# Four copies per head pair moved from GpSimd to VectorE in a fused attention and MLP-mixer kernel

## The chip, the cores and the metric

The kernel runs on one core of one Trainium2 chip. The metric is the device time of one execution in microseconds (us), smaller is better. The times quoted are medians of several executions; the profiled span is about 2 us shorter than the time of the same execution.

The engines of a core that matter here are TensorE (PE in the profile: matmuls; PEld: its weight loads), VectorE (DVE), ScalarE (ACT), GpSimd (POOL), which in this kernel also issues all input transfers, and the DMA engines that carry them out. Each engine has its own list of instructions, whose order is set when the program is built.

## The reference, cut to what matters

```python
# attention: 4 batches, 8 heads, 768 positions, head size 64; 8 global keys, window of 96
scores = q @ k.transpose(0, 1, 3, 2) / sqrt(D)
keep = is_global | is_local                  # key < 8, or 0 <= query - key < 96
scores = where(keep, scores + bias, -1e9)    # bias: -slope[head] * distance
a = softmax(scores);  x = a @ v              # reshaped to (4, 768, 512)
# mixer
u  = x + (x^T @ U @ V)^T                     # low rank 32 over positions
out = u + relu(u @ w_ch1) @ w_ch2            # 512 -> 2048 -> 512
```

Inputs and output are float32; the kernel computes in float16.

## The kernel before

The kernel takes two heads of one batch together, so there are 16 pairs. Of the 768 x 768 scores it computes only 128 x 128 blocks: six on the diagonal (from `kT`, the transposed keys) and five next to it (from `kP`). `kP` is a copy of `kT` whose first 32 columns of each block are overwritten with the first 32 keys, so that one matmul covers the previous block and the global keys. `vp` is the same for the values. Each is made by two copies, all four on GpSimd:

```python
            kT = qkp.tile([P, NSB, P], FP16, name="kT", tag="kT")
            nc.vector.tensor_copy(kT.rearrange("p n c -> p (n c)"), tp)        # from PSUM
            kP = qkp.tile([P, NPB, P], FP16, name="kP", tag="kP")
            nc.gpsimd.tensor_copy(kP[:, :, G:P], kT[:, 0:NPB, G:P])
            nc.gpsimd.tensor_copy(
                kP[:, :, 0:G], kT[:, 0:1, 0:G].broadcast_to((P, NPB, G))
            )
# ... (in mask(i), after the products with the exponential mask)
        nc.gpsimd.tensor_copy(vp, vh[:, :, 0:NPB])
        nc.gpsimd.tensor_copy(vp[0:G], vh[0:G, :, 0:1].broadcast_to((G, 2, NPB, D1)))
```

All inputs are converted from float32 to float16 by their transfer, which GpSimd issues:

```python
    def load_pair(i):                       # 2 transfers each of q, k, v
        # ...
                nc.gpsimd.dma_start(stg[:, :, hi], src[b, 2 * hp + hi].rearrange(...))
        # ...
    load_pair(0)
    # ... constants; load_pair(1); constants
    load_pair(2)
    load_pair(3)
    # ... u16, v16w (the low-rank weights)
    for c in range(NDC):
        nc.gpsimd.dma_start(w1_16[:, c], w1v[:, c])
    load_pair(4)
    for c in range(0, NJC, 2):
        nc.gpsimd.dma_start(w2_16[:, c:c + 2], w2v[:, c:c + 2])
    load_pair(5)
    # ... then one load_pair(i + 6) per step of the main loop
```

The main loop overlaps, per step, the low-rank mix of one pair, the attention of the next, and the scores of the one after. When all four pairs of a batch are done, that batch's MLP matmuls are queued and fill TensorE's gaps in the later steps. A scheduler sets the final order on every engine. In the names of the profile, `qkst` is a staging tile of q or k, `v_81` the values, `sc` scores, `ob` the attention output, `hps` and `cps` the two MLP products, `w_16_79` and `w_16_80` the MLP's weights.

The softmax here doesn't subtract the row's maximum and nothing guards it: scores larger than these inputs give would overflow.

## Time and profile before

| | before |
|---|---|
| time, median of 2 runs | 336.53 us (336.28 to 336.78) |
| profiled span | 334.3 us |
| TensorE busy | 263.7 us (79%) |
| VectorE / ScalarE / GpSimd busy | 114.4 / 132.1 / 126.5 us |

The first view gives the busy time of each engine in stretches of the span that I chose at events: until the first score matmul, until the scores of pair 2, until the MLP matmuls start in bulk, and the rest. After the length of the stretch come the busy times (with counts) of TensorE, its weight loads, VectorE, ScalarE and GpSimd, the granted TensorE clock (as a share of its full rate), the time that the transfers' packets took as a share of the 16 DMA engines' time (the times of packets are added up, so it can exceed 1), and GB/s. The clock column also says 1.00 where the trace has no record of the clock, which is so for the first three stretches.

```profile
core 0: us, PE busy (x) PEld busy (x) DVE busy (x) ACT busy (x) POOL busy (x), PEclk, DMA share, GB/s
0.00:50.81 50.81, 3.20 (x24) 2.47 (x25) 3.47 (x11) 4.69 (x9) 41.75 (x64) 1.00 1.43 143
50.81:68.76 17.95, 11.00 (x119) 8.39 (x120) 10.67 (x23) 8.28 (x15) 15.71 (x22) 1.00 1.33 85
68.76:108.96 40.20, 31.08 (x270) 20.95 (x271) 19.09 (x47) 18.09 (x32) 23.41 (x33) 1.00 0.79 51
108.96:334.30 225.34, 218.45 (x1668) 117.17 (x1667) 81.12 (x176) 100.98 (x210) 45.60 (x68) 1.00 0.29 42
```

Read the TensorE column against the length. In the first 50.81 us TensorE works 3.2 us. In the last 225.34 us it works 218.45: there TensorE is the bound, and only there.

The timeline shows what the first stretch waits for (start, duration, engine, line and operation; in brackets the idle time of the engine before it and what ended it). These are the first eviction of `kT`, one of the transfers, the first `kP` and the first score matmul.

```profile
9.48 0.56 DVE L182 COPY kT<-tp 128x768 f16<-128x768 f16 x1 [0.89 <-PE tp L170]
...
32.41 0.82 POOL L100 DMA_DIRECT2D v_81<-in_v_dram  x1 [1.59 <-DMA w_16_79<-in_moe_w_ch_dram]
...
49.90 0.60 POOL L184 COPY kP<-kT 128x480 f16<-128x480 f16 x1
...
50.81 0.71 PE L206 MATMUL sc<-qT,kP 64*128 64x128 f16 x9 [36.76 <-POOL kP L185]
```

`kT` of pair 0 is there at 10.04 us, and GpSimd makes `kP` of it at 49.90. Apart from four short mask operations (11.95 to 13.06 us), GpSimd was not computing in the meantime: in its fixed order, the transfers of pairs 0 to 5 and of all weights stand ahead, and some of these wait for earlier transfers to land, as the bracket at 32.41 us says. (By the trace the issues use eight semaphores in turn: those held up from 29.99 us on wait for the transfer eight before them, and at most eight are in flight.) The list of waits gives the total (us, number of waits, longest):

```profile
PE sc L206 <- POOL kP L185: 44.9, 7, 36.8
```

In the third stretch the same thing happens at a smaller scale, once per pair:

```profile
88.92 0.56 DVE L182 COPY kT<-tp 128x768 f16<-128x768 f16 x1 [1.35 <-PE tp L170]
...
89.12 1.66 POOL L94 DMA_DIRECT2D qkst<-in_k_dram  x2
...
90.75 0.62 POOL L184 COPY kP<-kT 128x480 f16<-128x480 f16 x1
91.28 0.35 POOL L185 COPY kP<-kT 128x160 f16<-128x160 f16 x1
...
91.68 0.71 PE L206 MATMUL sc<-qT,kP 64*128 64x128 f16 x9 [1.35 <-POOL kP L185]
```

`kT` is ready at 89.48, but GpSimd is issuing two k transfers until 90.78 and finishes `kP` at 91.63; TensorE was idle 1.35 us. The four groups of copies, with total busy us and mean ns of one:

```profile
L232 POOL COPY vp_82<-v_81 128x650 f16<-128x650 f16 x16 | 12.1, 758 | 1.3 <-PE ob L252 1.3
L233 POOL COPY vp_82<-v_81 32x650 f16<-32x650 f16 x16 | 12.1, 754 | 0.4
L184 POOL COPY kP<-kT 128x480 f16<-128x480 f16 x16 | 9.9, 621 | 49.5 <-DVE kT L182 49.5
...
L185 POOL COPY kP<-kT 128x160 f16<-128x160 f16 x16 | 5.6, 352 | 0.0
```

### The profile page before, as it was taken

Reading aid. Unit: us, or ns where it says so; the run is one execution under the profiler, and the core shown is the slowest. Engines: PE = TensorE matmul, PEld = TensorE weight load, DVE = VectorE, ACT = ScalarE, POOL = GpSimd, SP = SyncE. Lnnn points to the kernel's source line nnn. Section 1 sums busy time; section 2 is a strip of 40 time slices with the busy share of each in tenths; the row PEclk is TensorE's granted clock in tenths of the full one; section 3 lists DMA queues with packets and bytes.
Section 4 is the critical chain, followed back from the end, with each engine's and each line's share of the span. In section 5 each row is a group of like instructions: output and inputs, shape, how many; then the busy total and the mean of one; then the engine's idle time right before and its main releaser. Section 6 shows DMA issues by size and latency. Waiting matters only on the chain.

```text
span 334.3 us, 5123 instructions
## 1 busy us (share of the span) xinstructions
PE 263.7 (79%) x2080; PEld 149.0 (45%) x2080; DVE 114.4 (34%) x255; ACT 132.1 (39%) x265; POOL 126.5 (38%) x185
## 2 busy tenths in 40 slices
PE   0200006667688999999999999999999999999995
PEld 0200004545455556554455654555655554555442
DVE  0300004744544433355452434556342353100111
ACT  0320005353344485714447672415576521377100
POOL 8997579757645527143614140210201000000000
PEclk9999999999999999999999999999999999999999
DMA  9999999889749659258907160011000011100021
GB/s 70 96 120 184 181 205 116 53 55 73 48 33 64 40 32 59 14 65 102 113 32 49 9 42 33 31 65 63 2 0 2 2 63 63 65 0 0 33 92 65
DMA packets 82326, 20.34 MB, mean 61 GB/s; under 512 B 76640, under 2 KB 78720, under 8 KB 82304
## 3 DMA queue, kind: packets, MB, share of 16 engines
q0 software_dynamic: 78848, 13.74, 52.3%
q1 hardware_dynamic: 3456, 6.29, 5.1%
q8 instruction: 16, 0.26, 0.3%
q14 instruction: 6, 0.05, 0.1%
HBM read 27.46 MB, written 6.29 MB: 101 GB/s over the span
## 4 chain that ended last, share of the span: by engine, by line
PE 61%; POOL 16%; ACT 9%; DMA 6%; issue 4%; DVE 3%; POOLq 0%; ACTq 0%
PE cps L348 25%; PE hps L329 22%; POOL qkst L94 7%; PE sc L206 5%; ACT htr L335 4%; POOL v_81 L100 4%; DMA w_16_79<-in_moe_w_ch_dram 3%; PE h_ps L294 3%; ACT ep L212 3%; DMA w_16_80<-in_moe_w_ch_dram 3%; PE tmp_ps L282 2%; PE tp L170 2%; DVE x_sb L299 1%; POOL kP L184 1%; ACT uu L303 1%
## 5 line engine op out<-in xcount | busy, mean ns | idle before, releaser
L329 PE MATMUL hps<-uT,w_16_79 128*128 128x384 f16 x512 | 97.8, 330 | 2.7 <-ACT htr L335 0.7
L348 PE MATMUL cps<-w_16_80,htr 128*128 128x512 f16 x384 | 91.1, 379 | 0.0
L335 ACT ACTIVATE htr<-hps 128x384 f16<-128x384 f32 x128 | 58.0, 497 | 48.2 <-PE hps L329 48.2
L212 ACT ACTIVATE ep<-sc 128x512 f16<-128x512 f32 (+1 forms) x96 | 49.1, 583 | 62.4 <-PE sc L206 62.4
L329 PEld LDWEIGHTS <-w_16_79 128*128 128x128 f16 x512 | 49.2, 97 | 38.8 <-issue 8.7
L224 DVE TENSOR_TENSOR ep<-ep,expb 128x640 f16<-128x640 f16 x64 | 29.7, 498 | 73.7 <-ACT ep L212 73.6
L348 PEld LDWEIGHTS <-htr 128*128 128x128 f16 x384 | 34.5, 98 | 36.7
L94 POOL DMA_DIRECT2D qkst<-in_q_dram x32 | 26.9, 856 | 62.9 <-PE tp L170 61.9
L206 PE MATMUL sc<-qT,kP 64*128 64x128 f16 x160 | 13.2, 251 | 45.5 <-POOL kP L185 44.9
L354 DVE TENSOR_TENSOR osb<-cps,x_sb 128x512 f32<-128x512 f32 x24 | 16.5, 689 | 57.7 <-PE cps L348 57.5
L206 PEld LDWEIGHTS <-kP 64*128 64x128 f16 x160 | 6.6, 106 | 54.8 <-POOL kP L185 47.5
L170 PE MATMUL tp<-ident_91,qkst 128*128 128x128 f16 x192 | 21.1, 256 | 10.9 <-POOL ident_91 L113 7.2
L94 POOL DMA_DIRECT2D qkst<-in_k_dram x32 | 26.8, 860 | 6.5 <-PE ob L252 3.3
L184 POOL COPY kP<-kT 128x480 f16<-128x480 f16 x16 | 9.9, 621 | 49.5 <-DVE kT L182 49.5
L100 POOL DMA_DIRECT2D v_81<-in_v_dram x32 | 26.7, 847 | 3.8 <-DMA w_16_79<-in_moe_w_ch_dram 1.9
L303 ACT ACTIVATE uu<-x_sb 128x768 f16<-128x768 f32 x16 | 13.5, 844 | 37.1 <-DVE x_sb L299 36.7
L170 PEld LDWEIGHTS <-qkst 128*128 128x128 f16 x192 | 15.9, 115 | 16.1 <-issue 11.5
L299 DVE TENSOR_TENSOR x_sb<-x_sb,h_ps 128x768 f32<-128x768 f32 x16 | 15.3, 955 | 19.6 <-PE h_ps L294 19.6
L206 PE MATMUL sc<-qT,kT 64*128 64x128 f16 x192 | 20.7, 251 | 0.1
L252 PE MATMUL ob<-v_81,ep 128*128 128x65 f16 x160 | 17.6, 209 | 0.0
L248 PE MATMUL ob<-vp_82,ep 128*128 128x65 f16 x160 | 16.9, 210 | 0.0
L182 DVE COPY kT<-tp 128x768 f16<-128x768 f16 x16 | 8.9, 558 | 22.1 <-PE tp L170 18.7
(103 smaller groups left out, 210.0 us busy)
## 6 DMA issues: line engine op xcount, KB each, us to landing
out_dram<-osb SPq DMA_DIRECT2D x24, 256.0 KB, 2.0
qkst<-in_q_dram POOLq DMA_DIRECT2D x32, 96.0 KB, 3.7
qkst<-in_k_dram POOLq DMA_DIRECT2D x32, 96.0 KB, 3.6
v_81<-in_v_dram POOLq DMA_DIRECT2D x32, 96.0 KB, 3.6
w_16_79<-in_moe_w_ch_dram POOLq DMA_DIRECT2D x4, 512.0 KB, 8.5
w_16_80<-in_moe_w_ch_dram POOLq DMA_DIRECT2D x8, 256.0 KB, 7.7
u_151<-in_moe_U_dram POOLq DMA_DIRECT2D x1, 48.0 KB, 3.9
v16w<-in_moe_V_dram POOLq DMA_DIRECT2D x1, 48.0 KB, 3.5
```

What stands on the lines that cost most here:

```text
L94: nc.gpsimd.dma_start(stg[:, :, hi], src[b, 2 * hp + hi].rearrange("(n p) d -> p n d", p=P),)
L100: nc.gpsimd.dma_start(v16[:, i % VR, hi, :, 0:D], v[b, 2 * hp + hi].rearrange("(n p) d -> p n d", p=P),)
L170: nc.tensor.matmul(tp[:, sb * P:(sb + 1) * P], stg[:, sb].rearrange("s h d -> s (h d)"), ident16, is_transpose=True, start=(sb == 0), stop ...
L206: nc.tensor.matmul(scs[hi][:, j * P:(j + 1) * P], lhsT, qT[r, t * P:(t + 1) * P], start=(j == 0), stop=(j == len(idx) - 1),)
L212: nc.scalar.activation(ep[:, hi, idx[0]:idx[0] + n].rearrange("p n c -> p (n c)"), scs[hi][:, 0:n * P], AF.Exp, scale=qk_scale,)
L224: nc.vector.tensor_tensor(blk, blk, expb[:, h, m:m + 1].broadcast_to((P, NPB, P)), ALU.mult)
L248: nc.tensor.matmul(ob[:, t], ep[:, hi, t - 1], vp16[:, i % 2, hi, t - 1], start=True, stop=False,)
L252: nc.tensor.matmul(ob[:, t], ep[:, hi, NPB + t - 1], v16[:, i % VR, hi, t], start=False, stop=True,)
L299: nc.vector.tensor_tensor(xp, xp, hps[:, 0:S].rearrange("p (n c) -> p n c", n=NSB), ALU.add)
L329: nc.tensor.matmul(hh[f][:, 0:HT], w1_16[:, dc, jt * P:(jt + 1) * P], uTs[b][:, dc, f * HT:(f + 1) * HT], start=(dc == 0), stop=(dc == NDC ...
L335: nc.scalar.activation(htr[:, jt, f * HT:(f + 1) * HT], hh[f][:, 0:HT], AF.Relu)
L348: nc.tensor.matmul(cps, htr[:, jc, tt * P:(tt + 1) * P], w2_16[:, jc], start=(jc == 0), stop=(jc == NJC - 1),)
```

## The change

The intent is to leave GpSimd nothing but transfers, so that no copy waits behind a transfer.

```diff
-            nc.gpsimd.tensor_copy(kP[:, :, G:P], kT[:, 0:NPB, G:P])
-            nc.gpsimd.tensor_copy(
+            nc.vector.tensor_copy(kP[:, :, G:P], kT[:, 0:NPB, G:P])
+            nc.vector.tensor_copy(
                 kP[:, :, 0:G], kT[:, 0:1, 0:G].broadcast_to((P, NPB, G))
             )
 ...
-        nc.gpsimd.tensor_copy(vp, vh[:, :, 0:NPB])
-        nc.gpsimd.tensor_copy(vp[0:G], vh[0:G, :, 0:1].broadcast_to((G, 2, NPB, D1)))
+        nc.vector.tensor_copy(vp, vh[:, :, 0:NPB])
+        nc.vector.tensor_copy(vp[0:G], vh[0:G, :, 0:1].broadcast_to((G, 2, NPB, D1)))
```

## The prediction

This was written before the changed kernel had run.

> **What bounds the kernel now.** Three stages, by the table of engine time per stretch. (1) 0 to 50.8 us: TensorE is busy 3.2 us. (2) 50.8 to 109: attention pairs 0 to 4, one per 11.46 us, TensorE busy 42.1 of 58.2 us. (3) 109 to 334.3: MLP matmuls fill the gaps, TensorE busy 218.4 of 225.3 us and the bound.
>
> Stage 1 is no lack of data. By the timeline kT of pair 0 is ready at 10.0 us, of pair 1 at 14.7, but kP (GpSimd) starts at 49.9: GpSimd works in order, and ahead of kP stand the transfers of pairs 0 to 5 and all weights, which from about 29 us wait for earlier ones to land. The waits view names it: the score matmul waited 36.8 us for kP. In stage 2 kP stands behind two k transfers (kT ready 89.5, kP 91.6 us).
>
> **What the change does.** It takes 64 copies off GpSimd (per pair 0.62 + 0.35 + 0.76 + 0.75, in all 39.7 us) and adds 64 to VectorE (34% busy). The Trainium skill ("VectorE: DVE Perf Modes", the perf-mode tier table) gives an fp16 SBUF copy 4 elements a cycle. This trace has no such copy; its fp32 one (128x128, 217 ns) fits that page's 2 a cycle plus about 150 cycles. With that fixed part I estimate 0.28 + 0.19 + 0.33 + 0.33 = 1.1 us per pair, 18 in all. The transfers keep their order until 50 us, then have fewer gaps. TensorE's order moves little.
>
> **On the critical path.** Stage 1: kP(0) by 10.6 us, scores at once; the masks' table on ScalarE ends at 17.3 as before, exponentials of pairs 0 and 1 by 23, attention-times-value 23.5, normalisation 25, low-rank mix 27 (its weights issued 22.7, landing about 3.9 later). Scores of pair 2 start at about 32 us, not 68.8. Stage 2: going through one period with measured durations, kP is ready 1.4 us sooner, but the normalisation waits for two copies more and exponentials go ahead of x16: 10.2 us per pair instead of 11.46. Scores of pair 5 at 32 + 3 x 10.2 = 62.7 us (before 103.1), MLP from 68.6 (before 109). Transfers of pairs 4 and 5 should land near 37 and 53 us, in time. Stage 3 stays 225.3, less 1.5 for gaps where kP stood behind transfers (159 to 164 us). Sum: 68.6 + 223.8 + 2.2 (time over span) = 294.6.
>
> **Prediction: 295 us, 8 in 10 between 287 and 307.** Faster by over 2%: 0.96; within 2%: 0.03; slower: 0.01.
>
> **What would show it.** The long wait for kP is gone; scores of pair 0 start near 11 us, of pair 2 near 32; period 10.2 us; MLP from 69 us; TensorE's idle time falls by 41 us, its busy time stays 264; VectorE's busy time rises by 18 us.
>
> **What would make it wrong.** (a) The skill ("SBUF — State Buffer", Who interferes with whom) says a two-port VectorE copy and GpSimd exclude each other, and that issuing transfers suffers. Here the 217 ns copy ran inside a GpSimd issue undelayed, so I expect little; were it total, copies and issues of 0.85 us would stretch and early transfers slip. (b) The copies miss the fast mode (0.65 us for vp): 5 us more. (c) Later transfers land late, and TensorE, in order, stalls ahead of stage 3. (d) VectorE's longer queue delays evictions in stage 3, where each microsecond of TensorE counts. (e) A lower granted clock once TensorE works without pause.

## The result, and the profile after

| | before | after |
|---|---|---|
| time, median of 2 runs | 336.53 us | 295.70 us (295.11 to 296.29) |
| ratio | | 0.8787 (95% interval 0.8706 to 0.8867) |
| TensorE busy / idle in the span | 263.7 / 70.6 us | 262.6 / 31.9 us |
| VectorE busy | 114.4 us | 132.3 us |
| GpSimd busy | 126.5 us | 89.9 us |
| scores of pair 0 / 2 / 5 start | 50.8 / 68.8 / 103.1 us | 12.3 / 32.6 / 64.2 us |
| MLP matmuls start in bulk | 108.96 us | 69.26 us |
| from there to the end of the span | 225.34 us | 225.24 us |

A ratio is the mean time of one kernel's runs over that of the other's of the same rounds, so it is not quite the ratio of the medians. The idle time of TensorE is the span less its busy time.

The stretches between the same events as before:

```profile
core 0: us, PE busy (x) PEld busy (x) DVE busy (x) ACT busy (x) POOL busy (x), PEclk, DMA share, GB/s
0.00:12.27 12.27, 2.32 (x18) 1.83 (x19) 2.09 (x6) 1.28 (x1) 11.22 (x21) 1.00 1.26 80
12.27:32.60 20.33, 12.39 (x125) 9.06 (x125) 13.37 (x38) 10.63 (x22) 18.17 (x27) 1.00 1.50 138
32.60:69.26 36.66, 28.60 (x272) 20.47 (x271) 24.47 (x65) 17.83 (x33) 28.18 (x36) 0.98 1.74 161
69.26:294.50 225.24, 219.33 (x1670) 117.89 (x1668) 92.34 (x212) 100.81 (x209) 32.36 (x40) 0.99 0.37 47
```

The whole gain, 334.3 - 294.5 = 39.8 us of span, lies ahead of the MLP: its start moves by 108.96 - 69.26 = 39.7 us. The last stretch keeps its length to 0.1 us, although VectorE now works 92.34 us in it instead of 81.12. The early timeline (pair 0's `kT`, its first `kP` copy, the q transposes of pair 1, pair 0's scores):

```profile
9.46 0.56 DVE L182 COPY kT<-tp 128x768 f16<-128x768 f16 x1 [0.89 <-PE tp L170]
10.06 0.44 DVE L184 COPY kP<-kT 128x480 f16<-128x480 f16 x1
...
11.54 0.80 PE L170 MATMUL tp<-ident_91,qkst 128*128 128x128 f16 x6 [2.11 <-DMA qkst<-in_q_dram]
...
12.27 0.71 PE L206 MATMUL sc<-qT,kP 64*128 64x128 f16 x9
```

`kP` starts 0.04 us after `kT` is done. The scores then wait for a different thing: TensorE's order has pair 1's q transposes first, and these waited 2.11 us for their transfer. The line that answers to the third stretch of before:

```profile
39.82 2.82 POOL L155 DMA_DIRECT2D w_16_80<-in_moe_w_ch_dram  x4
...
40.67 0.56 DVE L182 COPY kT<-tp 128x768 f16<-128x768 f16 x1 [1.19 <-PE tp L170]
...
41.26 0.31 DVE L184 COPY kP<-kT 128x480 f16<-128x480 f16 x1
...
41.49 0.47 DVE L185 COPY kP<-kT 128x160 f16<-128x160 f16 x1
...
42.01 0.71 PE L206 MATMUL sc<-qT,kP 64*128 64x128 f16 x9
```

While GpSimd issues weight transfers, `kT` ends at 41.23, both copies at 41.96, and the scores start at 42.01, with no idle time of TensorE named. The copies on VectorE:

```profile
L233 DVE COPY vp_82<-v_81 32x650 f16<-32x650 f16 x16 | 6.7, 425 | 0.1
L184 DVE COPY kP<-kT 128x480 f16<-128x480 f16 x16 | 6.7, 419 | 0.4
L232 DVE COPY vp_82<-v_81 128x650 f16<-128x650 f16 x16 | 6.4, 407 | 12.9 <-PE ob L252 8.4 <-DMA v_81<-in_v_dram 4.5
...
L185 DVE COPY kP<-kT 128x160 f16<-128x160 f16 x16 | 4.5, 280 | 0.1
```

Two things in these lines had not been foreseen. The means add to 1.53 us per pair, not 1.1. And `vp` (L232) now has idle time of VectorE ahead of it, 4.5 us of which ended with a transfer of v. That is one single wait:

```profile
52.00 0.55 DVE L317 COPY uT<-tpu 128x768 f16<-128x768 f16 x1
57.03 0.51 DVE L232 COPY vp_82<-v_81 128x650 f16<-128x650 f16 x1 [4.48 <-DMA v_81<-in_v_dram]
...
58.28 0.47 DVE L224 TENSOR_TENSOR ep<-ep,expb 128x640 f16<-128x640 f16 x1
58.67 0.27 DVE L286 CAST tmp_748<-tmp_ps 32x128 f16<-32x128 f32 x1
...
59.00 0.79 PE L294 MATMUL h_ps<-tmp_748,v16w 32*128 32x128 f16 x6 [3.32 <-DVE tmp_748 L286]
```

From 52.5 to 57.0 us VectorE stands still for a `vp` copy. It is the copy of pair 5: its v, the last of the early transfers, was issued at 49.3 and 50.7 us. The scheduler put this copy ahead of the masks (L224) of pair 4 and of the low-rank eviction (L286) of pair 3, whose inputs were there by 54.4 and 55.2 us. So TensorE, too, stood still: 3.32 us for that eviction. The scores follow each other at 32.60, 42.01, 51.42 and 64.23 us: 9.41, 9.41 and then 12.81 us.

### The profile page after: what moved, and what is told of

The parts are those of the page before. It is cut to its first block, busy times and chain, and to the rows that moved or that the text cites. A ratio compares the mean times of both kernels' runs of the same rounds, so it can differ in the third digit from the quotient of the medians.

```text
span 294.5 us, 5117 instructions
## 1 busy us (share of the span) xinstructions
PE 262.6 (89%) x2080; PEld 149.2 (51%) x2080; DVE 132.3 (45%) x319; ACT 130.6 (44%) x265; POOL 89.9 (31%) x121
## 4 chain that ended last, share of the span: by engine, by line
PE 67%; DMA 9%; POOL 9%; ACT 7%; DVE 4%; issue 2%; POOLq 0%; ACTq 0%; DVEq 0%
PE cps L348 28%; PE hps L329 27%; DMA w_16_79<-in_moe_w_ch_dram 4%; POOL qkst L94 4%; PE sc L206 3%; ACT htr L335 3%; DMA w_16_80<-in_moe_w_ch_dram 3%; POOL v_81 L100 2%; DMA v_81<-in_v_dram 2%; PE tpu L311 2%; DVE x_sb L299 2%; PE h_ps L294 2%; PE tmp_ps L282 2%; ACT ep L212 2%; PE tp L170 2%
## 5 line engine op out<-in xcount | busy, mean ns | idle before, releaser
L329 PE MATMUL hps<-uT,w_16_79 128*128 128x384 f16 x512 | 96.5, 330 | 2.0
L212 ACT ACTIVATE ep<-sc 128x512 f16<-128x512 f32 (+1 forms) x96 | 48.5, 582 | 41.1 <-PE sc L206 41.1
L224 DVE TENSOR_TENSOR ep<-ep,expb 128x640 f16<-128x640 f16 x64 | 28.9, 485 | 33.5 <-ACT ep L212 33.1
L206 PE MATMUL sc<-qT,kT 64*128 64x128 f16 x192 | 21.4, 244 | 4.0 <-ACT ep L212 3.9
L206 PEld LDWEIGHTS <-kT 64*128 64x128 f16 x192 | 11.5, 104 | 15.0 <-issue 13.1
L270 DVE TENSOR_TENSOR x_sb<-ob,rcp 128x384 f32<-128x384 f32 x32 | 16.2, 547 | 0.0
L248 PEld LDWEIGHTS <-ep 128*128 128x128 f16 x160 | 13.7, 108 | 4.4 <-issue 2.7
## 6 DMA issues: line engine op xcount, KB each, us to landing
w_16_79<-in_moe_w_ch_dram POOLq DMA_DIRECT2D x4, 512.0 KB, 10.2
```

Of the source, the lines that this page charges most:

```text
L206: nc.tensor.matmul(scs[hi][:, j * P:(j + 1) * P], lhsT, qT[r, t * P:(t + 1) * P], start=(j == 0), stop=(j == len(idx) - 1),)
L212: nc.scalar.activation(ep[:, hi, idx[0]:idx[0] + n].rearrange("p n c -> p (n c)"), scs[hi][:, 0:n * P], AF.Exp, scale=qk_scale,)
L224: nc.vector.tensor_tensor(blk, blk, expb[:, h, m:m + 1].broadcast_to((P, NPB, P)), ALU.mult)
L248: nc.tensor.matmul(ob[:, t], ep[:, hi, t - 1], vp16[:, i % 2, hi, t - 1], start=True, stop=False,)
L329: nc.tensor.matmul(hh[f][:, 0:HT], w1_16[:, dc, jt * P:(jt + 1) * P], uTs[b][:, dc, f * HT:(f + 1) * HT], start=(dc == 0), stop=(dc == NDC ...
```

## The experiments

Theory: the gain comes from leaving GpSimd's in-order queue, in which copies stood behind transfers; the speed of the copies hardly matters, since the MLP stage is bound by TensorE and takes 225 us whatever comes before it. Rival: VectorE's copies are faster (1.5 us per pair instead of 2.5), and the gain goes with the copy time moved. A second question is what the change costs: VectorE's time, the new wait for v, and the stretched copies. The times below are medians of four or five runs; "before" ran beside each at 336.7 to 337.0 us.

### Only kP moves

```diff
-            nc.gpsimd.tensor_copy(kP...   (both)
+            nc.vector.tensor_copy(kP...   (both); vp stays on GpSimd
```

> Only the two kP copies move to VectorE; the two vp copies stay on GpSimd, behind the transfers. Queue theory (the gain comes from leaving GpSimd's in-order queue of transfers): scores of pairs 0 and 1 start near 12 and 18 us as with the whole change, but the first attention-times-value matmul now waits for vp until about 51 to 53 us, so only some 5 us of the early gain and 1 to 2 us per pair later are kept: 323 to 331 us, the gains of the two halves do not add up. Speed rival (VectorE's copies are simply faster, 1.5 against 2.5 us per pair): a gain in proportion to the copy time moved, about 4/10 of 41 us, 318 to 321 us.

Measured 324.75 us, ratio 0.9639 (0.9613 to 0.9666). The scores of pair 0 and 1 started at 12.18 and 18.91 us, as with the whole change, and the first matmul that needs `vp` waited:

```profile
PE ob L248 <- POOL vp L233: 29.9, 1, 29.9
```

So the half that made the scores 38 us early gained 12 us, because the next step then waited in the same queue. The queue theory's range held; the rival's 318 to 321 did not.

### Only vp moves

```diff
-        nc.gpsimd.tensor_copy(vp...   (both)
+        nc.vector.tensor_copy(vp...   (both); kP stays on GpSimd
```

> Only the two vp copies move; kP stays on GpSimd. Queue theory: the score matmul still waits for kP until about 50 us, stage 2 gains at most 1 us per pair: 328 to 336 us. Speed rival: 6/10 of 41 us gained, 310 to 314 us.

Measured 335.85 us, ratio 0.9967 (0.9941 to 0.9993). The scores of pair 0 started at 51.92 us. This half moves 1.5 of the 2.5 us of copies per pair and gains 1 us. The halves gain 12 and 1 us, both together 41: each removes one of two waits that end at nearly the same time (in the kernel before GpSimd starts `kP` at 49.90 us and `vp` at 50.69), and only removing both lets the chain go on. The rival would have had them add up.

### The copies stay on GpSimd, the transfers come later

```diff
-    load_pair(2); load_pair(3); <u16, v16w, w1>; load_pair(4); <w2>; load_pair(5)
 ...  in the loop, after mask(i + 1):
+        if i == -1: load_pair(2); load_pair(3); <u16, v16w>
+        if i == 0: <w1>
+        if i in (2, 3): <half of w2>
+        if 0 <= i < NP - 4: load_pair(i + 4)
```

> All four copies stay on GpSimd, but the program issues the transfers of pair 2 onwards and of the weights inside the loop, after the copies they used to stand before; the same transfers and copies, no copy on VectorE. Queue theory: scores of pair 0 start near 13 us and most of the gain appears without VectorE: 297 to 312 us (some lost since copies still stand behind weight transfers here and there and the pair chain keeps its 11.5 us). Speed rival, or that only VectorE frees GpSimd's 40 us: 325 to 340 us.

Measured 303.65 us, ratio 0.9009 (0.898 to 0.9037): 33 us gained with no copy on VectorE, and the groups of copies unchanged (0.61, 0.35, 0.76 and 0.74 us). The order of the queue is enough for most of the gain. The timeline shows what is still missing (`kT` is L172 here, `kP` L174):

```profile
12.94 0.64 POOL L174 COPY kP<-kT 128x480 f16<-128x480 f16 x1
...
14.24 0.48 DVE L172 COPY kT<-tp 128x768 f16<-128x768 f16 x1
...
26.24 0.67 POOL L174 COPY kP<-kT 128x480 f16<-128x480 f16 x1
...
27.23 0.71 PE L196 MATMUL sc<-qT,kP 64*128 64x128 f16 x9 [3.14 <-POOL kP L175]
```

Pair 0's `kP` is made at 12.94 us, but pair 1's, whose `kT` was ready at 14.72, at 26.24: the transfers of pairs 2 and 3 and the small weights still stood ahead.

### The same program with the copies on VectorE

```diff
 (e3_gp_loads_later)
-            nc.gpsimd.tensor_copy(...   (all four)
+            nc.vector.tensor_copy(...
```

> The program of e3_gp_loads_later (transfers issued inside the loop) with the four copies on VectorE: against e3 only the engine of the copies differs. Queue theory: with the transfers no longer ahead of the copies the engine itself is worth little, what is left being kP behind single transfers and pair 1's scores (27.2 us in e3): 4 to 9 us, 295 to 300 us. Speed rival: the move to VectorE is worth most of its 41 us here too: under 285 us; or nothing at all, 302 to 305 us.

Measured 292.5 us, ratio 0.8692 (0.8671 to 0.8713). That is 11 us less than with GpSimd, more than the 4 to 9 expected, and 2.5 us below the range. The difference is there early: scores of pair 1 at 18.91 instead of 27.23 us, of pair 2 at 32.50 instead of 40.45 (8 us), MLP at 65.35 instead of 75.46. By these times some 8 of the 11 us are again the queue, of which e3 had left more than I counted: in e3 pair 1's `kP` still waited there. Another 2 us come by the start of the MLP, and 1.7 after it (the last stretch takes 225.0 us instead of 226.7). How much of that is the shorter copies is not separated.

### Pair 5's transfers ahead of the second weight matrix

```diff
 (kernel after)
+    load_pair(5)
     for c in range(0, NJC, 2):
         nc.gpsimd.dma_start(w2_16[:, c:c + 2], w2v[:, c:c + 2])
-    load_pair(5)
```

> The kernel after, with pair 5's six transfers issued before those of the second weight matrix. Theory: in the kernel after, VectorE's vp copy of pair 5 stands ahead of pair 4's masks and waits 4.5 us (52.5 to 57.0 us) for v of pair 5, and pair 5's period is 12.8 us instead of 9.4. With v there in time that wait goes, MLP starts near 66 us, and 2.5 to 4 us are gained: 291.5 to 293.5 us. Rival (the longer period comes from elsewhere, or the saved time is lost to TensorE-bound stage 3): within 1 us of the kernel after, 295 to 297 us.

Measured 292.92 us, ratio 0.8692 (0.8669 to 0.8715). The wait is gone:

```profile
52.18 0.55 DVE L317 COPY uT<-tpu 128x768 f16<-128x768 f16 x1
52.64 0.32 DVE L232 COPY vp<-v 128x650 f16<-128x650 f16 x1
...
54.63 0.49 DVE L224 TENSOR_TENSOR ep<-ep,expb 128x640 f16<-128x640 f16 x1 [1.00 <-ACT ep L212]
```

The copy now starts at 52.64, right after the eviction ahead of it, and the masks wait 1.00 us for ScalarE only. Pair 5's scores come 8.99 us after pair 4's instead of 12.81, MLP starts at 66.13 us, and the last stretch takes 291.2 - 66.13 = 225.1 us. The wait for v was worth what it looked to be worth.

### Each copy made twice

```diff
 (kernel after)
             nc.vector.tensor_copy(kP[:, :, G:P], kT[:, 0:NPB, G:P])
+            nc.vector.tensor_copy(kP[:, :, G:P], kT[:, 0:NPB, G:P])
 ...  the same for the other three
```

> The kernel after with each of the four VectorE copies made twice (same result): another 64 copies, about 20 to 25 us of VectorE time. Theory: VectorE's time counts only in the chain of stage 2, where the second kP copy delays the scores by 0.5 us or a little more per pair, and stage 3 stays 225 us: 297.5 to 301 us in all. Rival A (VectorE's time counts in full, so the change paid its 18 us somewhere): 312 us or more. Rival B (VectorE time costs nothing at all): 295 to 296.5 us.

Measured 300.06 us, ratio 0.8903 (0.887 to 0.8936): 4.4 us above the kernel after (4.1 above e9 below, which ran in the same rounds) for another 64 copies, inside the theory's range and far from 312. In the profiled run MLP starts at 70.98 us, 1.7 later than in the kernel after, and the last stretch takes 225.9 us. That run was the fastest of the four (298.66); where the slower ones lose 1 to 2 us more is not known.

### kP copied from PSUM

```diff
 (kernel after)
-            nc.vector.tensor_copy(kP[:, :, G:P], kT[:, 0:NPB, G:P])
+            nc.vector.tensor_copy(kP[:, :, G:P], <tp as (p, n, c)>[:, 0:NPB, G:P])
 ...  the same for kP[:, :, 0:G]
```

> The kernel after, but the two kP copies read the transposed k in PSUM instead of kT in SBUF[...]. Port theory (the stretching of these copies from 0.31 to up to 0.71 us and from 0.19 to up to 0.79 us comes from GpSimd's issues holding the shared port): each copy then has one length, near 0.41 and 0.26 us, also inside GpSimd's issues; the total time stays within 1.5 us of the kernel after, 294.5 to 297 us. Rival (they stretch for another reason, such as waiting for the instruction before): the spread of lengths stays as in the kernel after.

Measured 295.98 us, ratio 0.8787 (0.8764 to 0.8809), the kernel after's. The lengths of one copy (minimum, median, maximum in ns) in the kernel after:

```profile
L184 DVE COPY kP<-kT x16: 307/309/711, 10.1 to 214.3; 128x480 f16<-128x480 f16 x16
L185 DVE COPY kP<-kT x16: 184/193/785, 10.4 to 214.5; 128x160 f16<-128x160 f16 x16
```

and here:

```profile
L184 DVE COPY kP<-tp x16: 386/398/400, 9.9 to 213.6; 128x480 f16<-128x480 f16 x16
L185 DVE COPY kP<-tp x16: 219/231/231, 10.2 to 213.9; 128x160 f16<-128x160 f16 x16
```

With a PSUM source the copies have one length to within 14 ns, as the port theory expected: the Trainium skill ("SBUF — State Buffer", Who interferes with whom) says that VectorE's two-port modes share a port pair with GpSimd, and that a VectorE instruction with one SBUF input at most, outside those modes, does not contend. The trace of the kernel after points the same way for all four groups: 22 of its 64 copies are longer than the others of their group (over 0.34 us, or 0.2 for L185), and each of them overlaps a transfer issue of GpSimd; the 19 that overlap none, `vp` copies among them, all have the short length. (A PSUM source was not tried for `vp`.) It makes no difference in time here: the copies from PSUM vary less, but their median is longer (398 instead of 309 ns, 231 instead of 193).

### The low-rank weights earlier

```diff
 (e4_w2_late)
+    <u16, v16w>
     load_pair(2)
     load_pair(3)
-    <u16, v16w>
```

> e4_w2_late with the two small low-rank weights issued before pair 2 instead of after pair 3. In the kernel after the first low-rank matmul waited 3.3 us for them (to 26.5 us) while its other operand was ready at 24.7. Theory: some 1.8 us earlier from there on, all of it kept as stage 3 stays 225 us: 290 to 291.8 us. Rival (pairs 2 and 3, now 1.5 us later, or something else then ends last): as e4, 292.5 to 293.5 us.

Measured 292.8 us, ratio 0.87 (0.8673 to 0.8727): no gain over e4_w2_late, so the expectation failed. The scores of pair 2 to 5 did come earlier (pair 5: 59.06 instead of 60.59), but then:

```profile
DVE vp L232 <- DMA v<-in_v_dram: 2.3, 1, 2.3
PE h_ps L294 <- DVE tmp L286: 1.8, 1, 1.8
```

The hoisted `vp` copy, now of pair 6, waited 2.3 us for its v, which stood behind the second weight matrix, and TensorE waited 1.8 us for the low-rank eviction behind that copy. The MLP started at 65.48 us, only 0.65 earlier. The same wait had moved to the next pair.

### The constants earlier

```diff
 (e7_uv_early)
+    <identity, distances, ones column of v>; q and k of pair 0; <distance masks>; v of pair 0
-    load_pair(0); <identity, distances>; load_pair(1); <distance masks, ones column of v>
+    load_pair(1)
```

> e7_uv_early with the constants (identity, distance table, ones column of v) built before v of pair 0 instead of around pair 1. In the kernel after ScalarE's table of exponentials ended at 17.4 us and pair 0's exponentials only then went on, to 19.9. Theory: the table ends near 10 to 11 us, pair 0's exponentials near 16, and 2 to 4 us more are gained than by e7: 286.5 to 289.5 us; stage 3 still 225 us. Rival: the early stage is then bound by arriving pairs, and it gains under 1 us over e7.

Measured 293.05 us, ratio 0.8695 (0.8662 to 0.8728). This failed too. VectorE's `vp` copies waited 8.1 us for v in four places before 70 us, and MLP started at 65.87.

### Transfers in the order of their use

```diff
 (e7_uv_early and, for e12, e10_consts_first)
     for c in range(NDC):
         nc.gpsimd.dma_start(w1_16[:, c], w1v[:, c])
+        if c < 2:
+            load_pair(4 + c)
-    load_pair(4); load_pair(5); <w2>
 ...  in the loop, after load_pair(i + 6):
+            if i in (1, 2): <half of w2>
```

> e7_uv_early with the transfers of pairs 4 and 5 set between the chunks of the first weight matrix and the second weight matrix split behind pairs 7 and 8 (that is, as late as possible). In e7 VectorE's vp copy of pair 6 waited 2.3 us for v of pair 6, which came behind the second weight matrix, and the MLP started at 65.5 us though the scores of pair 5 were 1.5 us earlier than in e4. Theory (the same hoisted-copy wait, moved one pair on, ate e7's gain): with v earlier the wait goes, MLP starts near 64 us, stage 3 stays 225 us: 290 to 292 us. Rival (stage 3 grows by as much as the MLP starts earlier): as e7, 292.5 to 293.5 us.

> The same order of transfers with the constants of e10 first. In e10 VectorE's vp copies waited 8.1 us in four places for v behind weights, which ate its earlier start. Theory: without those waits the MLP starts near 61 to 63 us: 287 to 290.5 us. Rival: as e10, 291.5 to 293.5 us.

e11_interleaved: 291.3 us, ratio 0.8657 (0.8639 to 0.8675); MLP from 63.86 us, then 225.24. One wait of `vp` for v, of 2.2 us, was still there before 70 us. e12_interleaved_consts: 290.07 us, ratio 0.8616 (0.8599 to 0.8634); such waits add to 2.0 us there (8.1 in e10), MLP from 63.13 us, then 225.27. Both are in their ranges except that e12's MLP starts 0.1 us later than expected. e12 is the best version found: 5.6 us less than the kernel after. It also shows the limit of this road: in these runs the start of the MLP is nearly all that the transfers' order moved.

Across the profiled runs the start of the MLP explains the span: before 108.96, only kP 96.78, only vp 108.75, after 69.26, e4 66.13, e12 63.13 us, and the rest of the span is 225.1 to 225.7 us in each of them (226.7 with the copies on GpSimd and late transfers, 225.9 with doubled copies, 226.1 in e10).

## Why the prediction was right, point by point

- **Time.** 295 us predicted, 295.7 measured. The mechanism, the queue ahead of `kP`, is shown by e1 to e3: the same copies on GpSimd with the transfers behind them gain 33 of the 41 us. TensorE's idle time fell by 38.7 us, where 41 had been predicted.
- **Stage 1.** Scores of pair 2 at 32 us, measured 32.6. The first scores came at 12.3, not 10.6: I had overlooked that pair 1's q transposes stand ahead on TensorE and wait for their transfer. ScalarE had its table to finish until 17.4 us anyway, so little hung on it: in e9 they start at 10.54 us, those of pair 1 at 18.87 as here, and the time is the same.
- **Stage 2.** 10.2 us per pair predicted. Two pairs took 9.41, the third 12.81, together 31.63 us against 30.6. The number was nearly right by two errors: the undisturbed period was shorter than I worked out, and the named risk (c), late transfers, came true in a form I had not seen: VectorE waited first, for a copy that the change had put into its queue, and TensorE 3.32 us for VectorE. e4 shows its price, 2.8 us (295.7 to 292.9).
- **Stage 3.** I had taken 1.5 us off for gaps where `kP` stood behind transfers. That was wrong: the stretch is 225.24 us against 225.34. Fewer such waits did not shorten it. Which other waits took their place I did not follow up.
- **VectorE.** Busy time rose by 17.9 us, with 18 predicted, but the copies took 1.53 us each pair, not 1.1. Undisturbed ones came close to the estimates (0.31, 0.19, 0.32 and 0.32 us against 0.28, 0.19, 0.33 and 0.33); the rest is copies that stretched during transfer issues, for `kP` by the shared port (e9). Risk (a) was real, and as far as e9 tests it harmless. The agreement on 18 us is partly luck: the sum of the copies' lengths is 24.3 us, the lengths of neighbouring VectorE instructions overlap in the profile, and the masks (L224, L227) are together about 2 us shorter than before. Moving the copies causes this: between e3 and e8, which differ in the copies' engine alone, the masks also go from 35.6 to 33.4 us. How is open: of the six that are clearly lengthened in the kernel before, five overlap a GpSimd copy, but of the five in e3 three overlap only transfer issues.
- **Transfers.** They kept their order, as predicted, but not quite their times: the first v of pair 4 was issued at 31.73 instead of 29.99 us, for the first MLP weights landed later. In e1 it was 30.01, in e2 31.26. Whether the `vp` copies do that is left open; one profile each does not settle it.
- **Clock.** Risk (e) did not come. The profile's mean of 0.91 between 60 and 80 us is one stretch at 0.50, from 68.1 to 71.5 us, the same half rate that TensorE had before its first clock record (last section). Lasting full rate starts 2.2 us after the MLP's start here and 2.6 us after it in the kernel before, so it follows the earlier start and does not explain it.

## What to carry to other kernels

Ask of every small instruction on an engine that also issues transfers what stands ahead of it in that engine's order: here 40 us of a 336 us kernel were small copies, each under 0.8 us, standing behind transfers they did not need. Moving such work to another engine moves its waits there too, so look afterwards for the copy that now makes the new engine wait for data, and order the transfers by when their data is first waited for. When one stage is bound by TensorE, as the MLP is here, what counts most of the rest is how early that stage starts.

## What the Trainium skill lacked or had wrong

- "SBUF — State Buffer", Who interferes with whom: it says that of a two-port VectorE instruction and a GpSimd one the second fully blocks until the first has finished. A transfer issue of GpSimd, about 0.85 us, does not hold the port throughout: the `kP` copy at 14.69 us of the kernel after took 0.31 us inside an issue, while copies of 0.19 us took up to 0.79 in others. GpSimd's issues became 2 to 8% longer (on average q transfers from 856 to 876 ns, v transfers from 847 to 916); from e3 to e8 it was under 2%. The page has no figure for how long an issue holds the port.
- "VectorE: DVE Perf Modes", the perf-mode tier table, and on the same page "Side-by-side: where the cycles go": nothing wrong was found, but the page's times are for 2048 elements, and copies as small as these fit less well. Its 4 elements a cycle plus about 150 cycles of 0.96 GHz give estimates of 326 ns for 650 elements ((650 / 4 + 150) / 0.96), 281 for 480 and 198 for 160. Measured, undisturbed: 310 to 333, 307 to 310 and 193 to 194 ns; 480 elements from PSUM took 386 to 400.
- "TensorE: Matmul & The Clock Gate", What's actually happening: it tells of a half-rate and a full-rate state of the array, set by how busy it was. The traces show the two rates: where the clock is recorded as 1.00, MLP matmuls of 384 columns follow each other at 162 ns and transposes and low-rank matmuls of 128 columns at 56 (medians); where it is recorded as 0.50, at 320 and 107 (e4). What the page does not spell out is that a trace can have no record ahead of the first change, and that a mean over the records then shows 1.00. The first record is at 111.6 us in the kernel before and at 64.7 in the kernel after. Ahead of it matmuls of 128 columns follow each other at 107 ns in both, and of 384 at 320 and 295 (medians again): TensorE ran at half rate through the first three stretches of the views above, except for 64.7 to 68.1 us of the kernel after, which is recorded as 1.00. In the same way six matmuls of 128 columns took 0.82 us in the kernel before (no record, the q transposes at 85.1 us) and in e4 (0.50, the low-rank matmuls at 63.6 us), and 0.50 us in e7 (1.00, the same six at 61.5 us). What triggers the change, and how many microseconds the half rate costs the early stages, is not shown by these runs.
